# Silu as one ScalarE function, and a new dealt order for the first batch of an attention-plus-SwiGLU kernel

## The chip, the core and the metric

The kernel runs on one core of one Trainium2 chip. The metric is the device time of the whole program in microseconds (us), the median of several executions. The profile is of one execution; its span is about 2 us shorter than the timed figure. The profile names the engines PE (TensorE, matrix products), PEld (its weight loads), DVE (VectorE), ACT (ScalarE), POOL (GpSimd) and SP (the engine that issues most transfers). "L585" is line 585 of the kernel that is profiled; the same statement has another number in another version, and the text says which.

## The reference, cut to what matters

```python
# attention: x is (8, 8, 512, 64), state is (8, 8, 32, 64)
a  = softmax(x @ state^T / 8);   xread = a  @ state     # "tokens read"
a2 = softmax(state @ x^T / 8);   sread = a2 @ x         # "states read"
y  = concat(xread, sread) -> (8 * 544, 512)

# SwiGLU block on every row of y
xn   = y / rms(y) * rms_g
g    = xn @ w_gate                       # 512 -> 1536
silu = g * (1 / (1 + exp(-g)))
out  = (silu * (xn @ w_val)) @ w_out     # 1536 -> 512
```

The three weight matrices arrive as 64-bit floats. The kernel takes them apart and puts them together as 32-bit floats on the chip, in 18 pieces, while batch 0 already runs.

## The kernel before: the parts concerned

Each of the 18 weight pieces needs three ScalarE steps (stream `e`, the exponents) and four VectorE steps (stream `d`, the values). Both end in a `yield`, so that a string of letters can deal them out:

```python
ORDER = (
    "aaaaaaaaaaaaededaasaseaaeaesaaasaaaassasdaaasassaesaddedseadeddadaadaasaeaesadve"
    ...
    "dehuudeddedpedpeddepdedpeddpedepddpddpdppAAAAAAAAAApAApAAAAApAAApAAAAAAAAApAApAA"
    "pAAAApAApAApApAApppSSSSSSSSSSSSSS"
)
...
    streams = {"a": tokens_read(0), "s": states_read(0), "A": tokens_read(1), "S": states_read(1),
               "e": exponents(), "d": values(),
               "v": (step for mp in range(NM // 2) for step in own_weights(0, mp)),
               "h": of_batch_0(0), "t": of_batch_0(1), "u": of_batch_0(2),
               "p": project_as_ready(store_tokens(0))}
    with tc.manual_schedule(engines={PE, DVE, Activation}):     # names shortened
        for stream in ORDER:
            next(streams[stream])
```

`manual_schedule` keeps each engine's instructions in the order in which the letters put them (`h` gate and value products, `t` the nonlinear function, `u` the gating, `p` two of the four products that add one block of the hidden layer to the output). What follows in batches 1 to 7 is placed by the compiler's scheduler. Silu is built from a Tanh, and the gating takes two VectorE instructions:

```python
        def tanh():
            t.append(two.tile([P, S], F32, name="t", tag="g"))
            SE.activation(out=t[0][:, 0:n], in_=gp[:, 0:n], func=ACTF.Tanh, scale=0.5)   # L500
            yield
        def gated():
            VE.scalar_tensor_tensor(out=t[0][:, 0:n], in0=t[0][:, 0:n], scalar=1.0,      # L504
                                    in1=gp[:, 0:n], op0=ALU.add, op1=ALU.mult)
            yield
            VE.scalar_tensor_tensor(out=h[:, 0:n], in0=t[0][:, 0:n], scalar=0.5,         # L507
                                    in1=vp[0][:, 0:n], op0=ALU.mult, op1=ALU.mult)
```

After the dealt part come the weight sums and then batches 1 to 7. They use a scheme with seven products instead of eight, in `hidden_seven` (L540, gate and value) and `project_seven` (L631, output). Between these products the attention of the next batch is dealt by `some(n)`.

```python
    for b in range(1, B):
        steps = attention(b + 1) if b + 1 < B else state_norm()
        ...
        for mp, pair in enumerate(pairs):
            ...
            next(pair)
            some(2)                      # two attention steps behind each of the six pairs
        project_seven(S, store_tokens(b), lambda: some(5), lambda: prepare(b + 1))
```

## Time and profile before

| | before |
|---|---|
| time, median of 3 | 877.97 us (877.09 to 878.15) |
| span of the profiled run | 875.5 us |
| last weight piece done | 119.2 us |
| last output product of batch 0 done | 154.1 us |
| states begin | 811.7 us |

The prediction below shows the views that bound the kernel. The groups by shape (line, engine, operation, count, then busy us and mean ns, then idle time before and what ended it) have exactly one load of ScalarE's function tables:

```profile
L271 ACT ACT_TABLE_LOAD x1 | 1.3, 1283 | 1.9 <-issue 1.9
```

So Exp, Tanh, Square, Abs, Relu and Copy all run from one set of tables in the kernel before, with the one load of 1283 ns at 1.9 us.

### The profile page before, as it was taken

How to read it: one execution, taken by the hardware profiler on the slowest of the kernel's cores; microseconds unless marked ns; L12 is line 12 of the kernel's file. 1: busy time of each engine (PE TensorE's matmuls, PEld its weight loads, DVE VectorE, ACT ScalarE, POOL GpSimd, SP SyncE). 2: the span in 40 equal slices, each digit the busy share in tenths (PEclk: the TensorE clock that was granted, in tenths of full speed). 3: DMA queues.
4: the chain of work that ended last, by engine and by line, in shares of the span. 5: the costliest groups of instructions: out<-in, count | busy, mean ns of one | idle time of the engine just before them, and what ended most of it. 6: DMA issues, size and time to landing. Idle time of an engine off the chain costs nothing.

```text
span 875.5 us, 12065 instructions
## 1 busy us (share of the span) xinstructions
PE 829.4 (95%) x4806; PEld 607.5 (69%) x4806; DVE 470.0 (54%) x738; ACT 345.7 (39%) x571; POOL 150.7 (17%) x215
## 2 busy tenths in 40 slices
PE   5688889999999999999999999999999999999998
PEld 3333334667877777767876787777876787788886
DVE  4899993369225941585146822594158613651231
ACT  5787732564135421553046313642056313520110
POOL 0000001321123211321122112321132022300000
PEclk7798999999999999999999999999999999999999
DMA  9798800721243222420433124320242012311310
GB/s 282 231 314 326 297 0 7 237 98 52 61 133 113 80 52 97 145 97 4 121 121 104 45 62 133 116 77 1 85 157 97 1 59 94 144 42 37 109 48 25
DMA packets 61592, 94.11 MB, mean 107 GB/s; under 512 B 38752, under 2 KB 46432, under 8 KB 54624
## 3 DMA queue, kind: packets, MB, share of 16 engines
q1 hardware_dynamic: 59456, 92.81, 31.8%
q8 instruction: 38, 0.62, 0.3%
q10 hardware_dynamic: 2080, 0.52, 0.3%
q14 instruction: 18, 0.15, 0.1%
HBM read 78.12 MB, written 15.20 MB: 107 GB/s over the span
## 4 chain that ended last, share of the span: by engine, by line
PE 73%; DVE 18%; ACT 4%; issue 2%; DMA 2%; SPq 0%; POOL 0%; DVEq 0%; ACTq 0%
PE f L631 31%; PE f L540 23%; PE f L493 6%; PE pv L453 5%; PE f L585 2%; DVE ex L216 2%; DVE raw L213 1%; ACT sq L343 1%; DVE eS L304 1%; DVE sq L346 1%; PE at L269 1%; DVE w_m L221 1%; DVE m L302 1%; ACT e L378 1%; DVE m L372 1%
## 5 line engine op out<-in xcount | busy, mean ns | idle before, releaser
L540 PE MATMUL f<-aT_s,v 128*128 128x256 f32 x504 | 131.6, 394 | 0.1
L540 PEld LDWEIGHTS f<-aT_s,v 128*128 128x128 f32 x504 | 89.3, 189 | 49.2 <-issue 29.3
L631 PE MATMUL f<-wo,hb 128*128 128x256 f32 x540 | 121.6, 381 | 0.0
L631 PEld LDWEIGHTS f<-wo,hb 128*128 128x128 f32 x540 | 101.9, 191 | 15.4 <-ACT ot L651 1.9
L651 ACT COPY ot<-f 128x256 f32<-128x256 f32 x60 | 19.6, 375 | 191.5 <-PE f L631 191.5
L631 PE MATMUL f<-wt,hs 128*128 128x256 f32 x360 | 94.5, 409 | 0.0
L462 ACT COPY v<-pv 128x512 f32<-128x512 f32 x96 | 51.7, 591 | 105.8 <-PE pv L453 105.8
L540 PE MATMUL f<-aT_t,vs 128*128 128x256 f32 x336 | 87.2, 382 | 2.5 <-DVE g L559 2.3
L475 POOL TENSOR_TENSOR vs<-v 128x256 f32<-128x256 f32 x42 | 30.6, 728 | 318.3 <-ACT v L462 318.3
L631 PEld LDWEIGHTS f<-wt,hs 128*128 128x128 f32 x360 | 69.6, 202 | 16.4 <-issue 4.9
L540 PEld LDWEIGHTS f<-aT_t,vs 128*128 128x128 f32 x336 | 62.8, 190 | 15.1 <-POOL vs L478 6.5
L656 DVE TENSOR_TENSOR ot<-ot,f 128x256 f32<-128x256 f32 x45 | 17.1, 418 | 104.5 <-issue 52.8
L453 PE MATMUL pv<-w_m,stT_g 64*32 64x512 f32 x768 | 63.2, 618 | 7.7 <-DVE w_m L221 7.7
L555 DVE TENSOR_TENSOR g<-g,f 128x512 f32<-128x512 f32 x42 | 28.7, 683 | 77.3 <-PE f L540 71.6
L565 ACT ACTIVATE hb<-g 128x1024 f32<-128x1024 f32 x42 | 44.4, 1057 | 31.4 <-DVE g L559 31.4
L566 DVE SCALAR_TENSOR_TENSOR hb<-hb,g 128x1024 f32<-128x1024 f32 x42 | 51.5, 1226 | 7.3 <-ACT hb L565 7.3
L238 POOL TENSOR_TENSOR ri<-ss,mhalf 128x4 f32<-128x4 f32 x8 | 8.5, 1056 | 242.6 <-DVE ss L354 242.6
L493 PE MATMUL f<-aT_s,v 128*128 128x512 f32 x96 | 46.2, 637 | 3.4 <-ACT v L462 1.9
L585 PE MATMUL f<-wo,hb 128*128 128x512 f32 x96 | 44.7, 613 | 0.6 <-DVE t L504 0.6
L540 PE MATMUL f<-aT_t,v 128*128 128x256 f32 x168 | 43.1, 379 | 0.0
L540 PE MATMUL f<-aT_s,vs 128*128 128x256 f32 x168 | 43.1, 379 | 0.0
L493 PE MATMUL f<-xsT,w_m 128*128 128x256 f32 x192 | 41.6, 379 | 0.0
(112 smaller groups left out, 1233.4 us busy)
## 6 DMA issues: line engine op xcount, KB each, us to landing
w_m<-w_d SPq DMA_DIRECT2D x48, 1024.0 KB, 4.8
x_b<-in_x_dram SPq DMA_DIRECT2D x30, 256.0 KB, 4.1
out_dram<-ot SPq DMA_DIRECT2D x56, 128.0 KB, 1.8
raw<-in_moe_w_val_dram SPq DMA_DIRECT2D x6, 1024.0 KB, 8.3
w_d<-w_m SPq DMA_DIRECT2D x6, 1024.0 KB, 5.0
raw<-in_moe_w_out_dram SPq DMA_DIRECT2D x6, 1024.0 KB, 7.4
raw<-in_moe_w_gate_dram SPq DMA_DIRECT2D x5, 1024.0 KB, 5.8
raw<-in_moe_w_gate_dram SPq DMA_DIRECT2D x2, 512.0 KB, 5.4
```

The costliest lines, as they stand in the source:

```text
L216: VE.scalar_tensor_tensor(out=ex, in0=hi, scalar=-(1 << 31), in1=ex, op0=ALU.bitwise_and, op1=ALU.bitwise_or)
L453: TE.matmul(out=pv[e][Ns * j:Ns * j + Ns, :], lhsT=stT_g[b][D * e:D * e + D, j, :], rhs=w[D * e:D * e + D, j].rearrange("p m k f -> p (m k ...
L462: SE.copy(v[:, e].rearrange("p m k f -> p (m k f)"), pv[e])
L475: GE.tensor_tensor(out=vs[:, 0], in0=a21, in1=a22, op=ALU.add)
L493: TE.matmul(out=(vp[0] if k else gp)[:, 0:n], lhsT=lhs(i, k), rhs=r, start=(i == 0), stop=(i == len(rhs) - 1))
L540: TE.matmul(out=ps[:, i, :], lhsT=lhs[:, i, :], rhs=rhs, start=(start and i == 0), stop=True, skip_group_check=True)
L555: VE.tensor_tensor(out=g[:, :, 0, :], in0=g[:, :, 0, :], in1=ys, op=ALU.add)
L565: SE.activation(out=h, in_=gate, func=ACTF.Tanh, scale=0.5)
L566: VE.scalar_tensor_tensor(out=h, in0=h, scalar=1.0, in1=gate, op0=ALU.add, op1=ALU.mult)
L585: TE.matmul(out=op, lhsT=hb[:, m, P * r:P * r + P], rhs=wo[:, m, :], start=(m == 0), stop=(m == NM - 1))
L631: TE.matmul(out=ps[:, r, :], lhsT=lhs(k)[:, P * r:P * r + P], rhs=rhs(k), start=(start and r == 0 and k == 0), stop=(k == HM - 1), skip_gr ...
L651: SE.copy(kept[r], ps[:, r, :])
```

## The change

Its intent: take one VectorE instruction out of each gating step of batch 0 and of the states, by using the Silu function of ScalarE; and deal the first batch anew, so that batch 1's attention (`A`) runs inside batch 0's gate and value instead of behind the last weight piece. Batch 0's states read (`s`) moves behind the projection. The weight sums (`k`) and batch 1's first own weights (`w`) become streams of their own. Batches 1 to 7 keep Tanh.

```diff
 ORDER = (
-    "aaaaaaaaaaaaededaasaseaaeaesaaasaaaassasdaaasassaesaddedseadeddadaadaasaeaesadve"
     ...
-    "pAAAApAApAApApAApppSSSSSSSSSSSSSS"
+    "aaaaaaaaaaaeddeaaaeaaeaeaaaeaaaaaeaedaaaaaedadaddadadadaaaeaaedaeadvedadvavhehde"
+    "dhtdedheuedtdAvAeuAvdvhdAhdedehtdedhuedtedAvAuAdevdvhdAhededhdtedhuedtevdueAvdvh"
+    "AdhededhdtedhuedtevdueAvdvhAdAhdedhtdehuededtveduAvAdvhAAehAAAAAAhAAtehuedtdAeuA"
+    "ApAAeAdepdAdAdpAAdAdpAAAeApedAedpAAeddpedeAdpAepeddepdpddpddpdwwwpppkpkpkpkkpkpk"
+    "kpkpkkpksssSsSsSsssssSsSSsSssSSSSSSS"
 )
@@ tokens_read: the product with rms_g comes after the exponentials
-        VE.tensor_tensor(out=stT_g[b], in0=stT, in1=rms_g..., op=ALU.mult)
...
+        VE.tensor_tensor(out=stT_g[b], in0=stT, in1=rms_g..., op=ALU.mult)
+        yield
@@ hidden
-            SE.activation(out=t[0][:, 0:n], in_=gp[:, 0:n], func=ACTF.Tanh, scale=0.5)
+            SE.activation(out=t[0][:, 0:n], in_=gp[:, 0:n], func=ACTF.Silu)
...
-            VE.scalar_tensor_tensor(out=t[0][:, 0:n], in0=t[0][:, 0:n], scalar=1.0,
-                                    in1=gp[:, 0:n], op0=ALU.add, op1=ALU.mult)
-            yield
-            VE.scalar_tensor_tensor(out=h[:, 0:n], in0=t[0][:, 0:n], scalar=0.5, in1=vp[0][:, 0:n],
-                                    op0=ALU.mult, op1=ALU.mult)
+            VE.tensor_tensor(out=h[:, 0:n], in0=t[0][:, 0:n], in1=vp[0][:, 0:n], op=ALU.mult)
@@ start: rms_g is fetched ahead of the first weight piece
-    load_piece(0)
     nc.sync.dma_start(out=rms_g, in_=moe_rms_g...)
+    load_piece(0)
@@ streams
-               "p": project_as_ready(store_tokens(0))}
+               "p": project_as_ready(store_tokens(0)), "w": first_of_batch_1(),
+               "k": weight_sums()}
...  (the rest makes w and k streams: own_weights calls more_of_v, weight_sums yields after each sum)
```

More of the change, by code (lines that the diff above doesn't have):

```diff
@@ L22 @@
 ORDER = (
-    "aaaaaaaaaaaaededaasaseaaeaesaaasaaaassasdaaasassaesaddedseadeddadaadaasaeaesadve"
-    "aavdvdadeaededhtdeuhedeuhtdvvdvudedhuehtdedhuedehtudhedvevuvuddedeAhtdedhueudhtd"
-    "ehuudvevdvddedehtddehuedhtudvevuvddedhuehtdedhuedehtudhedvevuvuddedehtdedhueudht"
-    "dehuudeddedpedpeddepdedpeddpedepddpddpdppAAAAAAAAAApAApAAAAApAAApAAAAAAAAApAApAA"
-    "pAAAApAApAApApAApppSSSSSSSSSSSSSS"
+    "aaaaaaaaaaaeddeaaaeaaeaeaaaeaaaaaeaedaaaaaedadaddadadadaaaeaaedaeadvedadvavhehde"
[3 more added lines that the diff above has]
+    "kpkpkkpksssSsSsSsssssSsSSsSssSSSSSSS"
 )
@@ L259, in tokens_read @@
         VE.tensor_copy(stT, tp)
-        yield
-        VE.tensor_tensor(out=stT_g[b], in0=stT, in1=rms_g.unsqueeze(2).to_broadcast([P, 4, Ns]),
-                         op=ALU.mult)
         yield "step"
@@ L308, in tokens_read @@
             yield "step"
+        VE.tensor_tensor(out=stT_g[b], in0=stT, in1=rms_g.unsqueeze(2).to_broadcast([P, 4, Ns]),
+                         op=ALU.mult)
+        yield
         aT_s[b] = two.tile([P, 2, S], F32, name="aT_s")
@@ L462, in own_weights @@
             SE.copy(v[:, e].rearrange("p m k f -> p (m k f)"), pv[e])
-            yield
+            if e == 0:
+                yield
+        if b in aT_t:
+            more_of_v(b, mp)
+        yield
     def make_v(b, mp):
@@ L467, in make_v, with more_of_v @@
             pass
+    def more_of_v(b, mp):
         v, _ = v_sb[b, mp]
-        if b in aT_t:
-            vs = seven["vs"].tile([P, 3, 2, P], F32, name="vs")
-            v_sb[b, mp] = v, vs
-            a11, a12, a21, a22 = (v[:, e, :, k, :] for k in range(2) for e in range(2))
-            GE.tensor_tensor(out=vs[:, 0], in0=a21, in1=a22, op=ALU.add)
-            GE.tensor_tensor(out=vs[:, 1], in0=vs[:, 0], in1=a11, op=ALU.subtract)
-            GE.tensor_tensor(out=a21, in0=a11, in1=a21, op=ALU.subtract)
-            GE.tensor_tensor(out=vs[:, 2], in0=a12, in1=vs[:, 1], op=ALU.subtract)
+        vs = seven["vs"].tile([P, 3, 2, P], F32, name="vs")
+        v_sb[b, mp] = v, vs
+        a11, a12, a21, a22 = (v[:, e, :, k, :] for k in range(2) for e in range(2))
+        GE.tensor_tensor(out=vs[:, 0], in0=a21, in1=a22, op=ALU.add)
+        GE.tensor_tensor(out=vs[:, 1], in0=vs[:, 0], in1=a11, op=ALU.subtract)
+        GE.tensor_tensor(out=a21, in0=a11, in1=a21, op=ALU.subtract)
+        GE.tensor_tensor(out=vs[:, 2], in0=a12, in1=vs[:, 1], op=ALU.subtract)
     def hidden(m, n, lhs, rhs):
@@ L495, in products, with silu @@
                 yield
-        def tanh():
+        def silu():
             t.append(two.tile([P, S], F32, name="t", tag="g"))
-            SE.activation(out=t[0][:, 0:n], in_=gp[:, 0:n], func=ACTF.Tanh, scale=0.5)
+            SE.activation(out=t[0][:, 0:n], in_=gp[:, 0:n], func=ACTF.Silu)
             yield
         def gated():
-            VE.scalar_tensor_tensor(out=t[0][:, 0:n], in0=t[0][:, 0:n], scalar=1.0,
-                                    in1=gp[:, 0:n], op0=ALU.add, op1=ALU.mult)
-            yield
-            VE.scalar_tensor_tensor(out=h[:, 0:n], in0=t[0][:, 0:n], scalar=0.5, in1=vp[0][:, 0:n],
-                                    op0=ALU.mult, op1=ALU.mult)
+            VE.tensor_tensor(out=h[:, 0:n], in0=t[0][:, 0:n], in1=vp[0][:, 0:n], op=ALU.mult)
             if seven and m >= HM:
@@ L516, in gated @@
             yield
-        return products(), tanh(), gated()
+        return products(), silu(), gated()
     aT_t = {}
@@ L618, in weight_sums @@
                 VE.tensor_tensor(out=dst, in0=a, in1=b, op=ALU.subtract)
-            yield
+                yield
     def project_seven(n, store, between, prepare):
@@ L708, in of_batch_0, with first_of_batch_1 @@
             yield from parts_0[m][part]
+    def first_of_batch_1():
+        slot_sums(1)
+        yield from own_weights(1, 0)
     parts_0 = {}
@@ L712 @@
     load_x(0, nc.scalar, nc.sync)
+    nc.sync.dma_start(out=rms_g, in_=moe_rms_g.rearrange("(i p) -> p i", p=P))
     load_piece(0)
-    nc.sync.dma_start(out=rms_g, in_=moe_rms_g.rearrange("(i p) -> p i", p=P))
     for k in range(1, RAW_AHEAD):
@@ L726 @@
         for stream in ORDER:
+            if stream in "wk" and not seven:
+                early.close()
+                open_late()
             next(streams[stream])
@@ L730 @@
             pass
-    early.close()
-    open_late()
-    prepare(1)
     load_state(2)
@@ L739, in some @@
             next(steps, done)
-    sums = weight_sums()
-    for _ in sums:
-        pass
     for b in range(1, B):
```

## The prediction

The forecast's sum is the last piece at 119.2 - 1.3 + 1 = 119 us, batch 1 at 147 us instead of 159.9, and 877.97 - 13 = 865, written as 864.5. Where cuts are marked, statements are gone that no trace of this case showed: among them what the table loads cost ScalarE and its sum with them, and the time of the first rival, where ScalarE is the bound. At the 1283 ns of the one load in the trace, three loads are an estimated 3.8 us, which makes the 91 us of ScalarE about 95 of 105; that the fuller ScalarE costs 1 us more waiting was the author's estimate.

> **What bounds the kernel now.** I read the 40 slices first, then the busy time by stretch, then the chain of waits, then the timeline of the first 160 us. The page's slices (21.9 us each), in tenths:
>
> ```profile
> PE   5688889999999999999999999999999999999998
> DVE  4899993369225941585146822594158613651231
> ACT  5787732564135421553046313642056313520110
> PEclk7798999999999999999999999999999999999999
> ```
>
> From the eighth slice on TensorE is full and nothing else is. Only the first seven slices can give time, and there VectorE is the full engine up to about 130 us. Busy time by stretch (us, count in brackets; order PE, PEld, DVE, ACT, POOL, then clock, DMA share, GB/s):
>
> ```profile
> 11.00:36.00 25.00, 14.50 (x133) 9.07 (x133) 22.92 (x41) 19.27 (x30) 1.33 (x1) 0.66 0.85 263
> 36.00:81.00 45.00, 37.33 (x129) 14.34 (x130) 41.92 (x48) 34.83 (x41) 0.00 (x0) 0.88 0.89 307
> 81.00:119.20 38.20, 33.84 (x97) 14.44 (x95) 36.82 (x40) 27.53 (x29) 0.00 (x0) 1.00 0.63 233
> 119.20:154.10 34.90, 32.56 (x126) 15.46 (x127) 19.22 (x37) 9.13 (x19) 3.86 (x5) 0.95 0.03 10
> 159.90:811.60 651.70, 640.72 (x3923) 496.08 (x3924) 330.90 (x530) 240.78 (x426) 144.63 (x199) 0.99 0.26 87
> ```
>
> VectorE is idle 2.1, 3.1 and 1.4 us of the first three stretches: from 11 to 119 us it turns the weights from 64 to 32 bits (18 pieces), with batch 0's attention and gating dealt between. Then from 119 to 154 TensorE is full although the weights are ready. The chain of waits (start, length, what):
>
> ```profile
> 118.00 1.23 DVE wo L221
> ...
> 126.98 0.61 DVE m L302
> ...
> 131.59 0.86 PE at L325 x4
> 132.45 3.18 PE f L585 x4
> ...
> 138.83 5.35 PE f L585 x12
> 144.17 0.79 PE at L350 x8
> 144.96 3.54 PE f L585 x8
> 148.50 0.44 PE at L245 x4
> 148.94 5.15 PE f L585 x12
> 154.09 0.87 PE at L385 x8
> ...
> 159.91 0.44 PE f L540
> ```
>
> The reader sees three things done one after the other: the last weight piece (ends 119.2), then the weight sums and batch 1's attention (`at`) mixed with batch 0's output product (L585), and from 159.9 batch 1's gate and value (L540). Batches 1 to 7 and the states then run 651.7 and 41.4 us with TensorE at 98% and 100%. So the time is about 159.9 plus a tail that this change hardly touches.
>
> [...] The trace has one load in the whole kernel, 1283 ns, [...] Abs, Relu, Copy, Exp, Square and Tanh share one set here. [...] here Tanh and Copy of 128x512 from PSUM both take 586 ns, so I take 586 ns for Silu. [...] four L493 instructions at 36.5 us took 3.55 us (0.89 each), sixteen at 91.6 took 7.13 (0.446 each), and the granted clock is 0.66 and 0.88 before 81 us.
>
> **The change, part by part.**
>
> 1. Silu in batch 0. Tanh stays one ScalarE instruction; of the two VectorE ones (L504 and L507, mean 682 and 687 ns, 0.60 us each on the chain because neighbours overlap) one goes: 12 x 0.60 = 7.2 us less VectorE work before 119 us.
>
> 2. Silu in the states. 12 x 0.42 us off VectorE, which is busy 12.6 of 41.4 us there while TensorE has no gap: worth nothing.
>
> 3. Table loads. Reading the new order: exps of batch 0's attention, ten Silus, two exps of batch 1, two Silus, then exps of the two states reads; one more Silu set for the final states. That is the first load plus 5, three before the weights are done[...].
>
> 4. Batch 1's attention moved before the last weight piece. Its VectorE steps, summed by the rows (four passes of 0.61 for maximum and subtraction; two of sum 0.61, reciprocal 0.5, product 0.62; three adds of 0.65; rescale 1.2; small ones 0.7): 9.8 us. All 45 steps now stand ahead of the last conversion step, against one before.
>
> 5. Batch 0's states read moved behind the projection: 2.6 us of VectorE (two maxima, 1.2, and small ones) leave the full stretch.
>
> 6. The start. VectorE waited 5.04 us for rms_g at 6.0 to 11.06 us; the product with it now comes later, and the first weights landed by about 9.8 us (ScalarE's first Abs, 9.75, did not wait). About 1.3 us earlier. But the two maxima that filled the gap at 12.3 are gone.
>
> So VectorE's sum to the last piece is unchanged: -7.2 - 2.6 + 9.8 = 0.0. ScalarE's rises from about 86 to 91 by the rows (+8.4 attention, -3.0 states read)[...] of the some 105 us it has. That makes it nearly as full as VectorE, so I allow 1 us more waiting. **Last piece: 119.2 - 1.3 + 1 = 119 us.**
>
> After it: the order has 11 of the 24 projection steps left, against 16. One step is 4 instructions of 0.44 us. 11 x 1.76 = 19.4, plus batch 1's first own weights, 1.0 (16 of L453 in 1.02 to 1.1): 139.4. The attention's 7.5 us on TensorE (`at`, 119 to 154) are gone from here, and the weight sums, 12 x 0.60 = 7.2 us of VectorE, run beside the products. But TensorE takes on more before 119: five steps, 8.8, plus 7.5, against 38 us of gaps and half clock that it had there; I allow 2 us of backlog: 141.5. Then two states reads: 8 transposes 0.87, 64 small products 1.03, one transpose 0.2, so 2.1 each, 4.2; and 1.5 us of waiting, since both use the same exp buffer. **Batch 1 starts at 147 instead of 159.9: 13 us less.** 877.97 - 13 is 865; I write 864.5, leaning a little to fewer gaps, as the order was dealt for that.
>
> **Rivals.**
>
> - ScalarE becomes the bound. [...] Against: in the trace the other ACT work waits up to 2.9 us for VectorE pieces, so there is slack. [...]
> - TensorE becomes the bound of the first 140 us. For: it has some 109 us of full-clock work up to the end of the projection, and ran at 0.66 to 0.88 clock to 81 us. Against: its gaps there belong to VectorE's pace. If it falls 6 us behind, the time is 868 to 870.
> - The gaps close: VectorE's 6.6 us of idle time fall to 3, there is no backlog, and the states reads hide in batch 1's products. Then batch 1 starts near 139 and the time is 857.
> - Batch 2's input comes late: its buffer is freed only by batch 0's states read, now at some 143 us rather than 23. Against: it is needed for steps spread over a batch of some 93 us (651.7/7). At most 1 to 3 us.
>
> **Range and chances.** Centre 864.5; the rivals span 857 to 870, so 857 to 872 holds it 8 times in 10. Two per cent is 17.6 us, 860.4: it takes most of the third rival, 0.23. Slower by 2% has no mechanism of that size, 0.01.
>
> **What would show it.** VectorE's last conversion of `wo` near 119; six table loads, three before it; 44 instructions of L585 after it; the first product of batch 1 near 147; from there about 652 us to the states, unchanged. Wrong would be: Silu in the same set as Exp (fewer loads), waits of conversion steps on ScalarE of over 5 us, TensorE idle between 119 and 147, or a longer batch 1 for its late input.

## The result, and the profile after

The changed kernel took 867.75 us (median of 4 runs, 867.21 to 868.93), against 877.53 us of the kernel before in the same rounds. The ratio is 0.9891, with a 95% interval of 0.9874 to 0.9908. Ratios here are the mean time of one kernel's fast runs over the mean time of the other's fast runs of the same rounds, so they are not quite the ratio of the medians quoted. The prediction was 864.5 in a range of 857 to 872, with "within 2%" at 0.76. The 9.8 us gained are less than the 13 that it forecast.

The 40 slices of the page, now 21.7 us each:

```profile
PE   4698999999999999999999999999999999999998
DVE  4799994586136921595147723592168513651021
ACT  6798843553146412552056213641155313520110
```

TensorE and ScalarE are fuller than before from the third slice on (9, 8, 9, 9 and 9, 8, 8, 4, against 8, 8, 8, 8 and 8, 7, 7, 3): batch 1's attention now runs there. VectorE reads 9 from the third to the sixth slice, as before. The busy time by stretch (PE, PEld, DVE, ACT, POOL, granted clock, DMA share, GB/s):

```profile
36.00:81.00 45.00, 42.36 (x172) 17.53 (x172) 40.70 (x44) 40.66 (x50) 0.00 (x0) 0.95 0.88 319
81.00:123.40 42.40, 38.28 (x151) 17.04 (x149) 40.88 (x50) 29.42 (x33) 1.39 (x1) 1.00 0.49 178
123.40:143.00 19.60, 19.60 (x62) 8.60 (x47) 14.63 (x20) 5.05 (x9) 8.96 (x8) 1.00 0.19 72
```

From 36 to 81 us PE, DVE and ACT are now 94, 90 and 90% busy. In the kernel before they were 83, 93 and 77%. Behind the last weight piece, which here ends at 123.4 us, TensorE has no gap at all. The chain of waits after the change:

```profile
122.90 1.02 PE pv L453 x16
123.92 19.08 PE f L585 x44
...
143.87 0.43 PE f L540 x2
...
151.84 6.32 PE f L540 x28
...
167.94 6.32 PE f L540 x28
```

The 44 remaining output products follow each other without a break, and the weight sums have left the chain. Batch 1 starts properly at 151.84, where its first run of 28 products begins; in between its first eight products are mixed with the two states reads. A good mark to compare by is the third such run. It starts at 167.94 here, and in the kernel before, by the same view, at 179.01:

```profile
179.01 6.32 PE f L540 x28
...
811.73 41.44 PE f L493 x192
```

So the front became 11.07 us shorter. The last line is the states' first products, which in the changed kernel stand at

```profile
802.31 41.44 PE f L498 x192
```

That is only 9.42 us earlier, the whole difference of the spans (875.5 and 866.1). **1.65 us were given back between 168 and 802 us, where the change moves nothing but one small VectorE product (with rms_g, in `tokens_read`).** Where to look is in the output products that follow the attention's squares, in the chain of batch 1, before and then after:

```profile
217.78 5.72 PE f L631 x26
```

```profile
206.71 7.41 PE f L631 x26
```

The same 26 products took 1.69 us longer. The granted clock (the column behind the POOL entry) in that stretch of the changed kernel says why:

```profile
203.00:206.60 3.60, 2.29 (x16) 1.81 (x14) 3.20 (x5) 1.08 (x3) 0.00 (x0) 1.00 0.08 18
206.60:210.00 3.40, 3.40 (x11) 2.78 (x12) 0.16 (x1) 0.00 (x0) 1.02 (x1) 0.64 0.02 5
210.00:213.40 3.40, 3.40 (x15) 2.92 (x14) 0.96 (x1) 0.65 (x2) 0.00 (x0) 0.86 0.00 0
```

TensorE was 1.3 us idle (2.29 busy of 3.60, waiting for VectorE's sums of the squares), then its clock was halved for 3.4 us (0.36 and 0.14 of two 3.4 us stretches are missing, together half of one; taken by 0.5 us, the clock is 1.00 up to 207.5, 0.50 from 208.0 to 210.5, and 1.00 again from 211.0). Such a stretch is called a clock spell below. Batches 1 to 6 all have this place. By the length of these 26 products, 7.3 to 7.4 us or 5.72, four of the six were hit in the profiled run of the kernel before, and five after the change.

The table loads are as the prediction read them from the order. Two groups of the changed kernel, ahead of Silu (L504) and of the exponentials of the tokens read (L304); the others are ahead of the first copy and of the states exponentials:

```profile
L504 ACT ACT_TABLE_LOAD x3 | 3.8, 1283 | 1.4 <-PE f L498 1.4
...
L304 ACT ACT_TABLE_LOAD x1 | 1.3, 1283 | 0.0
```

Two more groups have one load each, so there are six, all of 1283 ns, against one in the kernel before: Silu is not in the set that serves Exp and Tanh. Square needs no load beside either: four Squares of batch 1 ran from 102.6 to 104.7 us, between the Silu load at 91.5 and the next load at 125.1. Of Silu's three, two lie before the last weight piece and one in the states stage. Between the last exponential and the Silu behind the switch, in the chain of the changed kernel, there is nothing but the load and 0.04 us (91.51 to 92.83 is 1.32 us, the load 1.28):

```profile
90.36 1.15 ACT eS L304 x2
...
91.53 1.28 ACT L504
92.83 0.61 ACT t L504
```

What the prediction missed is the end of the last weight piece: 123.4 us, not 119. VectorE's waits up to then (who waited for whom, us in total, times, longest), first of the kernel before, from 11 us:

```profile
DVE t L504 <- ACT t L500: 2.5, 2, 1.3
...
DVE w_m L221 <- DMA w_d<-w_m: 0.7, 1, 0.7
```

and of the changed kernel, from 9.7 us:

```profile
DVE m L299 <- PE at L293: 2.1, 1, 2.1
DVE hb L508 <- PE f L498: 2.0, 1, 2.0
DVE w_m L221 <- DMA w_d<-w_m: 1.5, 1, 1.5
DVE aT_s L360 <- PE at L245: 1.3, 1, 1.3
DVE ss L354 <- PE at L350: 0.9, 1, 0.9
```

The first list makes 4.7 us with two more waits of 0.8 and 0.7; the second makes 9.5 us with four more of 0.2 to 0.6. VectorE's work is nearly the same: it was busy 102.5 us up to the last piece's end, against 101.7. All its idle time, named or not, rose from 6.5 to 11.2 us.

### The profile page after: what moved, and what is told of

Same layout as the page of the kernel before. It is cut to its first block, busy times and chain, and to the rows that moved or that the text cites. A ratio compares the mean times of both kernels' runs of the same rounds, so it can differ in the third digit from the quotient of the medians.

```text
span 866.1 us, 12042 instructions
## 1 busy us (share of the span) xinstructions
PE 824.3 (95%) x4806; PEld 606.6 (70%) x4806; DVE 462.1 (53%) x714; ACT 351.4 (41%) x576; POOL 154.7 (18%) x215
## 4 chain that ended last, share of the span: by engine, by line
PE 79%; DVE 12%; ACT 5%; issue 2%; DMA 1%; SPq 0%; POOL 0%; DVEq 0%; ACTq 0%
PE f L631 31%; PE f L540 23%; PE f L498 7%; PE pv L453 5%; PE f L585 5%; PE at L266 2%; ACT sq L343 1%; DVE sq L346 1%; ACT e L378 1%; DVE eS L301 1%; PE at L336 1%; PE at L350 1%; DVE m L299 1%; PE at L325 1%; DVE g L559 1%
## 5 line engine op out<-in xcount | busy, mean ns | idle before, releaser
L631 PE MATMUL f<-wo,hb 128*128 128x256 f32 x540 | 122.7, 383 | 0.0
L631 PEld LDWEIGHTS f<-wo,hb 128*128 128x128 f32 x540 | 103.0, 193 | 15.7 <-ACT ot L651 1.9
L651 ACT COPY ot<-f 128x256 f32<-128x256 f32 x60 | 19.6, 375 | 193.2 <-PE f L631 193.2
L453 PE MATMUL pv<-w_m,stT_g 64*32 64x512 f32 x768 | 61.3, 609 | 5.9 <-DVE w_m L221 5.9
L585 PE MATMUL f<-wo,hb 128*128 128x512 f32 x96 | 42.5, 596 | 1.5 <-DVE wo L221 1.5
```

The source lines that it names most:

```text
L453: TE.matmul(out=pv[e][Ns * j:Ns * j + Ns, :], lhsT=stT_g[b][D * e:D * e + D, j, :], rhs=w[D * e:D * e + D, j].rearrange("p m k f -> p (m k ...
L585: TE.matmul(out=op, lhsT=hb[:, m, P * r:P * r + P], rhs=wo[:, m, :], start=(m == 0), stop=(m == NM - 1))
L631: TE.matmul(out=ps[:, r, :], lhsT=lhs(k)[:, P * r:P * r + P], rhs=rhs(k), start=(start and r == 0 and k == 0), stop=(k == HM - 1), skip_gr ...
L651: SE.copy(kept[r], ps[:, r, :])
```

## The experiments

Three theories had to be told apart. **A**: VectorE sets the pace up to the last weight piece, so its work and its waits there decide. **B**: ScalarE, with batch 1's attention and the table loads on it, or TensorE, sets that pace. **C**: the 1.7 us given back come from the clock spells, which have nothing to do with the change. Twelve kernels ran. The kernel before took 878.6 and 878.4 us; e9 to e12 ran on another chip and it took 877.5, so runs are compared by their ratio to it as well.

| run | last weight piece done, us | time, us | ratio to before |
|---|---|---|---|
| before | 119.2 | 877.53 | 1 |
| the change | 123.4 | 867.75 | 0.9891 |
| e1 Silu in the old order | 115.6 | 876.34 | 0.9982 |
| e2 new order with Tanh | 129.4 | 874.73 | 0.9960 |
| e3 no switch of tables (wrong result) | 123.4 | 866.79 | 0.9869 |
| e4 the change, one attention step behind the last pair | 122.2 | 853.49 | 0.9716 |
| e7 before, with the edit of e4 | 120.8 | 864.01 | 0.9834 |
| e8 e1 with the edit of e4 | 115.1 | 861.09 | 0.9805 |
| e9 e2 with the edit of e4 | 129.5 | 860.34 | 0.9805 |
| e5 e4 with four weight buffers | 125.6 | 856.06 | 0.9745 |
| e6 e4 with the first gating later | 122.5 | 853.15 | 0.9714 |
| e10 e4, half products (wrong result) | 122.2 | 854.09 | 0.9735 |
| e11 e4, short Relu (wrong result) | 124.3 | 853.40 | 0.9725 |
| e12 e4, short first step (wrong result) | 122.7 | 854.67 | 0.9740 |

The second column comes from one profiled execution of each kernel. Kernels with the same front differ in it by 1.2 and 1.6 us (the change and e4; before and e7), so smaller differences there mean nothing.

### e1: Silu alone, in the old order

```diff
 # kernel before
-            SE.activation(..., func=ACTF.Tanh, scale=0.5)
+            SE.activation(..., func=ACTF.Silu)
-            VE.scalar_tensor_tensor(... add, mult)
-            yield
-            VE.scalar_tensor_tensor(... mult, mult)
+            VE.tensor_tensor(out=h[:, 0:n], in0=t[0][:, 0:n], in1=vp[0][:, 0:n], op=ALU.mult)
 # ORDER: every first of the two u letters of a block taken out
```

> The kernel before, its order kept, with Silu and one VectorE instruction per block in place of two (every first of the two gating steps taken out of the order). Theory (VectorE sets the pace up to the last weight piece): 12 x 0.60 = 7.2 us leave it, table loads give back about 1, so the last conversion of wo ends near 113 instead of 119.2, the 35 us of TensorE behind it stay, and the time is 871 to 873. Rival (ScalarE or TensorE sets that pace): the last conversion moves by under 2 us and the time is 876 to 878.

The last piece ended at 115.6, so 3.6 us of the 7.2 arrived (in the later pair e7 and e8 it is 5.7). The time scattered from 873.7 to 878.0 us, against a width of 1.7 to 1.9 us for the change and the kernel before, with a median of 876.34: a miss. The profiled run, 873.72, was the fastest of the four; what the other three lost was not recorded, and clock spells are only a guess. This is why the comparison was done again in e8 without the spells.

### e2: the new order alone, with Tanh

```diff
 # changed kernel
-            SE.activation(..., func=ACTF.Silu)
+            SE.activation(..., func=ACTF.Tanh, scale=0.5)
-            VE.tensor_tensor(out=h..., op=ALU.mult)
+            VE.scalar_tensor_tensor(... add, mult)
+            VE.scalar_tensor_tensor(... mult, mult)
```

> The changed kernel with Tanh and the two VectorE instructions put back into each gating step. Theory: VectorE carries 7.2 us more before the last weight piece, which ends near 130 instead of 123.4; three table loads go, worth under 1; the time is 873 to 875. Rival (in the new order ScalarE with its loads is the tighter engine): the last piece ends near 125 and the time is 868 to 870.

The last piece ended at 129.4, 6.0 us later, and the time was 874.73, 7.0 us more (6.1 by the ratios). In the new order most of VectorE's 7.2 us of extra work reaches the end, as A says.

### e3: no switch of tables

```diff
 # changed kernel; a wrong result on purpose
-            SE.activation(..., func=ACTF.Silu)
+            SE.activation(..., func=ACTF.Tanh)
```

> The changed kernel with Tanh written where Silu stands: a wrong result on purpose, the same instructions and sizes, no switch of tables. Theory (the loads fall into ScalarE's waits and cost VectorE only the 0.7 us of idle time seen beside the two loads at 89 and 91 us): one table load left, the last conversion ends near 122.5 instead of 123.4, time 866.5 to 868. [...]

The time was 866.79, within the theory's range, and the last piece ended at 123.4, as with the loads and not at 122.5. In this run VectorE's first maximum started 1.1 us later (14.09 against 12.97 us) and TensorE's granted clock was 1.00 from 9.7 to 36 us (0.63 in the change), so something up to about 1 us may have been won back in front of the last piece. The median is 1.0 us below that of the change, and 1.9 by the ratios, whose intervals overlap. So this run does not fix what the loads are worth: some 2 us at most. Three loads of 1283 ns that stalled the conversion in full would, without them, have put the last piece near 119.6 us (an estimate, 123.4 less 3.8); it ended at 123.4.

### e4: one attention step behind the last pair

```diff
 # changed kernel
-            some(2)
+            some(2 if mp + 1 < len(pairs) else 1)
         project_seven(...)
```

> The changed kernel, but in batches 1 to 7 only one attention step instead of two behind the last gate-and-value pair, so that the row sums of the squares (128x1 products) stand behind 8 more output products on TensorE. Theory: TensorE's wait of about 3.3 us less some small work before those products is followed in 6 of 7 batches by a stretch at lower granted clock, 7.41 us for 26 output products instead of 5.72; without the wait the lower clock does not come either: 6 x 1.7 + 6 x 1.3 = 18 us at most, time 850 to 858. Rival (the clock drops for another reason, or the wait moves elsewhere): still 7.41 us in most batches, time 864 to 869.

It took 853.49 us, ratio 0.9716 (0.9699 to 0.9734), **14.3 us less than the change by itself** (15.4 by the ratios), and, with e6 which adds to it, the fastest correct kernel. (The expectation says 6 of 7 batches; it is five of the six that have this place.) The chain of batch 1 shows the products that were slow, now in one run of 36 ahead of the row sums:

```profile
200.85 7.97 PE f L631 x36
208.82 0.80 PE at L350 x8
```

36 products in 7.97 us are 0.221 each; in a batch with a spell 26 took 7.41, or 0.285. The stretches from 195 to 210 us have TensorE full and the clock at 1.00 throughout, for instance:

```profile
201.00:204.00 3.00, 3.00 (x15) 2.64 (x15) 2.76 (x5) 1.93 (x4) 0.00 (x0) 1.00 0.10 22
```

Theory C is shown, and the sum closes. From the third run of products in batch 1 to the states it is 620.03 us here against 634.37. Each batch with a spell saves 2.67 us (a period of 95.35 us becomes 92.68), each without one 0.98 (93.66 becomes 92.68): 5 x 2.67 + 0.98 = 14.3.

### e7, e8, e9: the two parts of the change without the clock spells

The edit of e4, on the kernel before (e7), on e1 (e8) and on e2 (e9).

> The kernel before with one attention step instead of two behind the last gate-and-value pair: it takes the clock drops out of the comparison (the change itself has no part in them). Theory (the change is worth 11 us up to the start of batch 1, and the drops gave back 1.7 of that by chance): time 862 to 866, which is 10 to 12 us above the changed kernel with the same edit (853.5). Rival (the change costs something in batches 1 to 7 too): 859 to 861, under 8 us above.

> The previous run with Silu in the old order as well (one VectorE instruction per block less). Alone with the old clock drops this scattered from 873.7 to 878. Theory: of the 7.2 us of VectorE work taken away some 3.6 come back as waits for the value product, as in the first try (its last weight piece ended at 115.6 against 119.2), so batch 1 starts 3.5 to 5.5 us earlier and the time is 3.5 to 5.5 us under the previous run. Rival (VectorE was not the pace at all): under 1.5 us. Rival (it was the only pace): over 7.

> The new order with Tanh and two VectorE instructions per gating step, one attention step behind the last pair: the fourth corner beside 864.0 (neither), 861.1 (Silu alone) and 853.5 (both). Theory: the new order has no waits on the value product in which the second instruction could hide, so taking Silu out costs 6 to 7 us here against the 2.9 that Silu brought alone: 859.5 to 860.5. Rival (the two parts simply add): 853.5 + 2.9 = 856.4.

With that edit the scatter is 0.9 to 1.8 us. In e7 and e8 the spells are gone: the third runs of 28 products of batches 1, 5 and 6 are 92.67 us a batch apart, against 92.68 in e4. e7 took 864.01, so **the change by itself is worth 10.5 us** (864.01 - 853.49), as predicted for this run. The four corners are:

| | Tanh, two VectorE steps | Silu, one VectorE step |
|---|---|---|
| old order | 864.01 | 861.09 |
| new order | 860.34 | 853.49 |

Silu brings 2.9 us in the old order, a bit under its range (4.0 in the profiled runs, whose front varies by 1 to 1.5 us from run to run of one kernel), and 6.9 in the new one; the order brings 3.7 with Tanh and 7.6 with Silu. The parts do not add (2.9 + 3.7 = 6.6, not 10.5). The waits of VectorE in e8 say where Silu's 7.2 us went in the old order (L504 is there the gating, L493 the value product):

```profile
DVE hb L504 <- PE f L493: 4.6, 6, 1.9
```

The instruction that was removed had run while the value product was still being made. Without it VectorE stands there, six times, 4.6 us. The new order puts a step of batch 1's attention in such places. e9 is on another chip; by ratio to the kernel before it stands 0.0089 above e4, 7.8 us of 877.5. By the ratios Silu and the order bring 2.5 us each alone and 10.4 together, which is the same finding.

### e5 and e6: meant to take away two of VectorE's waits

```diff
 # e5, on e4
-W_BUFS = 3
+W_BUFS = 4
 # e6, on e4: the first u two conversion steps later
-  ...vhehdedhtdedheuedtdAvAeu...
+  ...vhehdedhtdedheedtduAvAeu...
```

> The changed kernel with one attention step behind the last pair (853.5) and four buffers for the rounded weights instead of three. Theory (VectorE's waits are what puts the last piece at 123 instead of 119): its wait of 1.5 us for a write to memory to end goes, the last piece and batch 1 come 1 to 1.5 us earlier, time 852 to 853. Rival (another engine sets the pace there and the wait is free): unchanged start of batch 1, 853 to 854.5.

> The changed kernel with one attention step behind the last pair, and the first gating step dealt two conversion steps later, so that VectorE does not stand 2.0 us before it waiting for the first value product, which runs at half clock. Theory: the last weight piece and batch 1 come up to 2 us earlier, time 851 to 852.5. Rival (the wait only moves to the next step, or TensorE sets the pace there): under 0.5 us, 853 to 854.

The theories of both missed; e6 came out in its rival's range, e5 in neither. With four buffers the last piece came 3.4 us later than in e4 and the time rose to 856.06. The list of VectorE's waits names gate and value products in place of the write:

```profile
DVE w_m L221 <- PE f L498: 4.1, 1, 4.1
```

The chain of waits contradicts this name. It goes over the write of a weight pair to memory in both runs, and VectorE starts 0.12 us after that write has ended. First e4, then e5:

```profile
73.30 4.97 DMA w_d<-w_m
...
78.39 1.23 DVE w_m L221
```

```profile
73.27 7.46 DMA w_d<-w_m
...
80.85 1.23 DVE w_m L221
```

So it is not shown that the fourth buffer took the wait away. The write took 2.5 us longer; why was not traced. In e6 the wait of 1.6 us before the gating disappeared, and the next cross-engine step waited instead:

```profile
DVE stT L259 <- PE at L256: 2.1, 1, 2.1
```

The time, 853.15, does not differ from e4.

### e10, e11, e12: one engine relieved at a time

All three give wrong results on purpose and keep the order of e4.

```diff
 # e10: TensorE, about 20 us less expected: half the contraction in batch 0's gate and value
-                                    [aT_s[0][:, e, :] for e in range(2)])
+                                    [aT_s[0][:, e, :] for e in range(1)])
 # e11: ScalarE, about 11 us less: the third exponent step on a quarter of the columns
-                SE.activation(out=ex, in_=ex, func=ACTF.Relu, ...)
+                w = ex.shape[1] // 4
+                SE.activation(out=ex[:, 0:w], in_=ex[:, 0:w], func=ACTF.Relu, ...)
 # e12: VectorE, about 7 us less: the first value step on a quarter of the columns
-                    VE.tensor_scalar(top, hi, 0xfffff, 0x100000, ...)
+                    w = top.shape[1] // 4
+                    VE.tensor_scalar(top[:, 0:w], hi[:, 0:w], 0xfffff, 0x100000, ...)
+                    top = top[:, 0:w].unsqueeze(1).to_broadcast([P, 4, w])
```

> A wrong result on purpose: batch 0's gate and value use only the first half of the contraction, about 20 us less TensorE work before the last weight piece; otherwise the changed kernel with one attention step behind the last pair (last piece ends at 122.2, time 853.5). Theory (VectorE sets the pace with some waits on TensorE early): the last piece comes 2 to 3 us earlier, time 850 to 852. Rival (TensorE sets the pace there): over 5 us earlier, time under 848.5.

> A wrong result on purpose: the third ScalarE step of each weight piece handles a quarter of its columns, some 18 x 0.64 = 11 us less ScalarE work before the last piece, same base (853.5). Theory: under 1.5 us earlier, time 852 to 854. Rival (ScalarE, 90% busy from 36 to 81 us with batch 1's attention on it, sets the pace): 4 us or more earlier, time under 849.5.

> A wrong result on purpose: the first VectorE step of each weight piece handles a quarter of its columns, some 18 x 0.4 = 7 us less VectorE work before the last piece, same base (853.5). Theory (VectorE sets the pace): the last piece comes 5 to 7 us earlier, and since TensorE is full behind it only part of that reaches the end: time 848 to 851. Rival (ScalarE or TensorE sets the pace): under 2 us earlier, time 852 to 854.

None moved the last piece by more than 0.1 us forward (122.2, 124.3 and 122.7 us against 122.2), and none was faster than e4 by more than 0.1 us (854.09, 853.40, 854.67 against 853.49). By the ratios, which allow for the other chip, all three are slower, by 0.8 to 2.1 us. e11 lies in its theory's range, e10 in neither of its two, and e12 0.7 us above its rival's. e10 took 12.9 us off TensorE's busy time up to 123.4 us (80.0 against 92.9) and not 20, for the clock was lower (0.84 from 36 to 81 us and 0.92 from 81 to 123.4, against 0.97 and 1.00). That refutes B, for ScalarE and TensorE each alone. But e12 also speaks against A in its simple form. VectorE was busy 7.1 us less up to 123.4 us (95.9 against 103.0), and its waits grew by as much:

```profile
DVE w_m L223 <- DMA w_d<-w_m: 4.0, 1, 4.0
DVE hb L510 <- PE f L500: 3.6, 4, 2.6
```

The first of them is the write again, longer than in e4 (7.22 us against 4.97). The chain of e12:

```profile
72.56 7.22 DMA w_d<-w_m
...
85.74 1.96 PE pv L455 x16
87.70 1.90 PE at L295 x8
89.60 7.91 PE f L500 x16
```

While VectorE stood there, TensorE ran out of work, waited 3.9 us for VectorE's next piece, and had a granted clock of 0.55 from 84.0 to 91.5 us, against 1.00 in e4. So e12 brought a clock spell of its own, and is not a clean test of VectorE's work.

Adding 7.2 us of VectorE work to this order costs 6 to 8 us (e2, e9); taking 7 away brought nothing. One reading is that the order is balanced: VectorE, ScalarE and TensorE are all near 90% busy, they hand work to each other in a fixed order, and when one is quicker it waits longer for the next. That is argued, not shown. The rival that no run relieved is the memory traffic, whose 16 engines are 0.88 to 0.94 busy from 36 to 81 us in e4, e10, e11 and e12. From 20 us on no engine of e4, e10, e11 or e12 waited for the load of a weight piece, but the write is on the chain of every kernel here, for 4.9 to 7.5 us. Whether the write or the mesh of waits fixes the 122 us **stays open**.

## Why the prediction was right or wrong

1. **What bounds the kernel: right.** All that the change does is in front of batch 1, and the states stage gained nothing: from its first product to the end both spans are 63.8 us.
2. **VectorE's sum unchanged: right to 0.9 us.** It was busy 102.5 us up to the last piece's end, against 101.7.
3. **The start 1.3 us earlier: right in size.** The first conversion step began at 9.73 us, the product with rms_g before it at 11.06. The missing maxima left the wait of 2.1 us in the list above.
4. **Table loads: right.** There are six, three of them between the first and the last weight piece. Silu took 582 ns, as assumed (586). The worth of the loads is some 2 us at most (e3). ScalarE was busy 90.1 us from 9.7 to 123.4 us with three loads in it, against the 91 of the forecast without them, and did not become the bound (e11).
5. **Last piece at 119 us: wrong, the main miss.** The step that failed is "I allow 1 us more waiting". VectorE's named waits rose from 4.7 to 9.5 us, and the piece was done at 123.4: 119.2 less 1.3 at the start, and 0.9 of work and 4.6 of idle time more. The longest waits are 2.1 us for the product before the first maximum, 2.0 for the first value product and 1.5 for the write. The first rival, ScalarE with its loads as the bound, is not the reason: without the loads (e3) the piece ended at 123.4 too. What the change did to VectorE's waits is shown; that they must grow when three engines are near 90% busy is not. In e6 a wait taken away came back elsewhere; e5 and e12 ran into a longer write.
6. **After the last piece: 22.5 us predicted, 19.6 measured.** (The terms make 22.4; the 141.5 is 0.1 too high.) The step that was mis-sized is the 2 us of backlog on TensorE: there was none, since the 44 products began at once, took 19.08 us, and the own weights 1.02. The 38 us of gaps and half clock set against it come to 32 by the prediction's own table (22.5 idle, 9.4 of lost clock).
7. **The states reads and the start of batch 1: right.** The end of the projection gained 11.1 us and the third run of products in batch 1 also 11.07, so nothing was lost in between. The late input of batch 2 cost nothing that can be seen.
8. **The tail unchanged: wrong by 1.65 us.** It was not foreseen that a wait of 1.3 us in batches 1 to 6, the same in both kernels, is followed by half clock in some batches (four of six before, five after) and not in others. The prediction took one trace's 651.7 us for a constant.
9. The sum. At the end of the projection 12.6 us were forecast (154.1 to 141.5); the last piece took 4.4 of them, the missing backlog and smaller terms gave 2.9 back: the 11.1 measured. The 0.3 us forecast for the states reads (5.5 against 5.8) did not come, and 1.65 went in the tail: the 9.4 of the spans. "Within 2%" came in. The third rival, the gaps close, did not. That the total is only 3.3 us off is in part luck, since the two largest errors, 4.4 and 2.9 us, had opposite signs.

## What to carry to other kernels

Where several engines are all near 90% busy (here TensorE 94, VectorE 90, ScalarE 90% from 36 to 81 us) and hand work to each other in a fixed order, do not forecast from the sum of the fullest one alone. Test with a run that takes work away from that engine, since work added and work removed need not count the same (here 7.2 us more on VectorE cost 6 to 8 us, 7.1 us less brought nothing), and look in its trace for what else moved (in e12 a longer write and a clock spell). Where an instruction runs while its engine would have waited, removing it brings a wait in its place (4.6 us of the 7.2 in e8), unless the order gives something else to do there (Silu brought 2.9 us alone, 6.9 with the new order). A short wait on TensorE can cost more than itself through its clock (here 1.3 us, followed by 1.0 us of 128x1 products and, in five of six batches, by 3.4 us at a clock of 0.50, which cost 1.69 us more): look at the clock column of otherwise identical stretches before explaining a difference between two versions. Here moving one step behind 8 more products (e4) was worth 14.3 us, more than the whole change.
